# Second-half x factors of a Strassen-like matmul: five of seven loaded, added and split at the turn instead of parked during the first half

## Chip, cores and metric

One NeuronCore of one Trainium2 chip runs the whole program; the other cores are not used. The metric is the device time of one execution in microseconds (us), smaller is better. The profile is one execution of the same program taken by the hardware profiler; its times below are us from the start of its span.

## The reference

The input x has 2048 rows of 512 values, all in fp32. Two branches are computed from it and mixed row by row by a gate.

```python
g = sigmoid((x * gate_w).sum(-1, keepdims=True))
# branch a: linear attention with 32 heads of 16
q, k, v = split_heads(x @ wqkv)                 # wqkv: 512 x 1536
pq, pk = phi(q), phi(k)                         # phi(t) = where(t > 0, t + 1, exp(t)) + 1e-6
kv = einsum("bhsd,bhse->bhde", pk, v); z = pk.sum over s
o  = einsum("bhqd,bhde->bhqe", pq, kv) / (einsum("bhqd,bhd->bhq", pq, z) + 1e-6)
a  = merge_heads(o) @ wo                        # wo: 512 x 512
# branch b: bilinear GLU, F = 1792
b  = ((x @ w_gate) * (x @ w_up)) @ w_down
out = g * a + (1 - g) * b
```

## The kernel before

**Split operands.** Every fp32 matrix that enters a matmul is written as a high part (an fp32r copy, made by ScalarE) and a low part (the rest, made by VectorE: source minus high part). One product then takes three matmuls: high by high, low by high and high by low (`mm3`). Making such a pair is called a split, and in the profile it is an ACT instruction that writes a tile ending in h, and a DVE instruction that writes one ending in l.

**Seven products instead of eight.** For each block of 128 columns of w_gate and w_up (or two such blocks of the q part of wqkv) the kernel computes two 128-column results over two chunks of 512 rows each, as a 2x2 block product in Strassen's manner: seven products of sums of weight blocks with sums of x blocks. The seven sums of x blocks are the x factors, numbered 1 to 7. A factor is 128 partitions x 2 x 512 values, 512 KB, and is held as a high and a low tile: factor 2 in the first half of the tiles xah and xal, 7 in their second half, 3 and 5 in the halves of xbh and xbl, and 1, 4 and 6 in tiles of their own (xc1h, xc1l and so on). Factors 2 and 5 are plain x blocks, the other five are a sum or a difference of two blocks (A1, A2, B1, B2, which are `xp[pair, 0]` to `xp[pair, 3]` in DRAM). A difference is made by a negation on ScalarE (`act(..., scale=-1.0)`) and an accumulating DMA, a sum by the accumulating DMA alone. Accumulating DMAs are issued by GpSimd (POOL), all others by SyncE (SP) with few exceptions.

**Pairs and units.** The 2048 rows are two pairs of 1024. A first phase computes k and the sums for kv and z for all rows and prepares the factors of the first pair. Then come 16 units for the first pair, numbers 0 to 15, and 16 units for the second, 16 to 31. A unit is one set of seven products, 14 of each 16 for the GLU and 2 for q. The seven products run on TensorE in the order 2, 3, 4, 1, 5, 6, 7, with PSUM banks Y, X, R and S as targets (bY, bX, bR, bS in the profile). Between them stand matmuls of the down projection (pdn), from unit 12 and 27 on those of the attention's output (po), and in units 1 to 3 small matmuls that fold kv into wo (pkv, pw). How many down jobs stand at each of four places of a unit is written in the table `shares`. The move from pair to pair, units 15 and 16, is called the turn.

**Order.** Each engine runs its instructions in program order. `later(n, place, fn)` hangs work at a place of unit n, and `do(n, place)` runs it. The places in their order within a unit: high (after product 2), low and e (after product 3), m and c (after product 4), d (before product 1), t (after product 1), s (after product 5), r (after product 6), end (after the unit). So a wait at one place holds up all that stands behind it on that engine.

**Weights.** `w_load(n + 3)` loads the raw weights of a unit (wr) at the end of unit n, `w_add` lets ScalarE copy and negate them and POOL add further blocks, and `w_high` and `w_low` split them (wch, wcl) one unit before they are used.

**The second pair's factors before the change.** While the first pair runs, half a factor at a time is loaded into a tile with the tag cb (three buffers; cbs in the profile) at place s of unit n, added at place c of unit n + 1, and at place e of unit n + 2 handed to `cb_split`. For factors 2, 3 and 4 that splits the half (cbh, cbs) and stores both parts in DRAM tiles xpark; for factors 1, 6 and 7 it stores the sum as it is in xsum. Factor 5 is copied from DRAM to DRAM. The halves run through units 0 to 13 in the order 2, 3, 4, 1, 6, 7. In unit 15, right after a product has used a factor for the last time, `reload` brings the next pair's: both parts of 2, 3 and 4, which are then ready, and the unsplit sums of 1, 5, 6 and 7, which are split in unit 16 at places m, c, t and s.

**Tiles of kv and wo.** In units 2 and 3 `wp_unit` makes four rows of the folded output weights (pw on TensorE, copied by ScalarE into wrow, stored in wraw), and `wp_minus` negates half a row in place and stores it. The wrow tiles share the tag ph, four buffers, with phq, the attention's feature map of a q unit (units 3 and 7).

Of the kernel before, what the change touches and what calls it, by code (L numbers as in the profile page):

```python
# [7 lines left out]
F32 = mybir.dt.float32  # L8
F32R = mybir.dt.float32r
AF = mybir.ActivationFunctionType  # L10
ALU = mybir.AluOpType
# [3 lines left out]
P = 128  # L15
S = 2048
D = 512
# [6 lines left out]
CH = 512  # L24
# [35 lines left out]
def gated_mix(ctx: ExitStack, tc, xt, xp, x, wqkv, wq, wq_add, wo, wgu, wgu_add, wdn, gate_w, out):  # L60
# [3 lines left out]
    dram = ctx.enter_context(tc.tile_pool(name="scratch", bufs=1, space=DRAM))  # L64
# [8 lines left out]
    def act(dst, src, func=AF.Copy, **kw):  # L73
        pin(nc.scalar.activation(dst, src, func, **kw))  # L74

    def tt(dst, a, b, op):
        pin(nc.vector.tensor_tensor(dst, a, b, op=op))  # L77
# [19 lines left out]
    def dma(dst, src):  # L97
        tc.keep_in_program_order(nc.sync.dma_start(dst, src))

    def dma_add(dst, src):  # L100
        tc.keep_in_program_order(nc.gpsimd.dma_start(dst, src, accum_op=ALU.add))  # L101
# [17 lines left out]
    xc = {2: [v[:, 0:2] for v in xa], 7: [v[:, 2:4] for v in xa],  # L119
          3: [v[:, 0:2] for v in xb], 5: [v[:, 2:4] for v in xb], **own}  # L120
# [10 lines left out]
    nc.gpsimd.affine_select(out=m3, in_=m3, compare_op=ALU.is_ge, fill=0.0, base=DH - 1,  # L131
                            pattern=[[DH, P // DH], [0, DH]], channel_multiplier=-1)

    xpark = {i: [dram.tile([P, 2, CH], F32, name=f"xpark{i}{v}") for v in "hl"] for i in (2, 3, 4)}
    xsum = {i: dram.tile([P, 2, CH], F32, name=f"xsum{i}") for i in (1, 5, 6, 7)}

    zpark = dram.tile([KT * KT, P, P // KT], F32, name="zpark")

# [10 lines left out]
    units = len(order) // NPAIR  # L149
# [27 lines left out]
    def w_low(n, part):  # L177
        if n < len(order):
# [5 lines left out]
    SUMS = {1: (A1, B2, 0), 3: (B1, B2, 1), 4: (A2, A1, 1), 6: (A1, B1, 0), 7: (A2, B2, 0), 2: (None, A1, 0),  # L184
            5: (None, B2, 0)}

    def x_load(tile_, pair, i, ks):
        dma(tile_, xp[pair, SUMS[i][1]][:, ks])

    def x_add(tile_, pair, i, ks):  # L190
        one, _, sub = SUMS[i]
        if sub:
            act(tile_, tile_, scale=-1.0)
        if one is not None:
            dma_add(tile_, xp[pair, one][:, ks])
# [4 lines left out]
    with tc.tile_pool(name="p1", bufs=2, reuse_waits="tile") as p1:  # L200
# [11 lines left out]
        for t in range(2 * CH // P):  # L212
            c, i = divmod(t, CH // P)
# [10 lines left out]
        for k in range(KT):  # L224
            raw = raw_of[k]
# [88 lines left out]
        part = phi_k(0, pk0[0])  # L314
        phi_split(*part)
        part = phi_k(1, pk0[1])
# [11 lines left out]
        def cb_load(i):  # L328
            cbs[i] = p1.tile([P, 2, CH], F32, tag="cbs", name="cbs", bufs=3)
            x_load(cbs[i], 0, i, slice(0, 2))  # L330
# [12 lines left out]
        for t in range(LEAD, NT + LEAD):  # L343
# [10 lines left out]
            part = phi_k(*late.pop(0)) if late else None  # L354
# [18 lines left out]
    p2 = ctx.enter_context(tc.tile_pool(name="p2", bufs=1, reuse_waits="tile"))  # L373
# [5 lines left out]
    def later(n, place, fn):  # L379
        at.setdefault((n, place), []).append(fn)  # L380

    def do(n, place):
        for fn in at.pop((n, place), []):
            fn()
# [4 lines left out]
    def down(k):  # L389
# [3 lines left out]
        while ojobs and ojobs[0][0] < passed[0]:  # L393
# [4 lines left out]


    shares = {2: (0, 1, 1, 1), 3: (1, 0, 1, 0), 4: (1, 0, 1, 0), 7: (1, 1, 0, 1), 8: (1, 1, 0, 1), 9: (1, 0, 1, 0)}  # L400
    shares.update({units: (1, 3, 1, 1), units + 1: (1, 1, 1, 0)})
    shares.update({units + m: v for m, v in ((2, (0, 1, 1, 1)), (3, (1, 0, 1, 0)), (4, (1, 0, 1, 0)),
                                             (5, (1, 1, 0, 1)), (6, (1, 1, 0, 1)), (7, (1, 0, 1, 0)),
                                             (15, (1, 1, 0, 1)))})

    def share(n):
        return shares.get(n, (1, 1, 1, 1))

    def unit(n, quad):

        wh, wl = wcs.pop(n)
        bank = {t: psum.tile([P, CH], F32, tag=t, name=f"b{t}") for t in "YXRS"}

        def reload(i):
            if n + 1 == units and i in xpark:
                for src, part in zip(xpark[i], xc[i]):
                    dma(part.bitcast(F32), src)
            elif n + 1 == units:
                hi, lo = xc[i]
                dma(lo.bitcast(F32), xsum[i])  # L420

                def split_there():
                    act(hi, lo.bitcast(F32))
                    tt(lo, lo.bitcast(F32), hi.bitcast(F32), ALU.subtract)

                later(units, {1: "m", 5: "c", 6: "t", 7: "s"}[i], split_there)

        def product(i, to, start=False):
            for k in range(2):
                ks = slice(k * P, (k + 1) * P)  # L430
                mm3(bank[to], (wh[:, SLOT[i], ks], wl[:, SLOT[i], ks]), [v[:, k] for v in xc[i]],
                    start and k == 0, k == 1, not start)
            reload(i)

        m2 = p2.tile([P, CH], F32, tag="t", name="m2")
        cross = p2.tile([P, 2, CH], F32, tag="cross", name="cross", bufs=2)
        product(2, "Y", True)
        act(m2, bank["Y"])
        do(n, "high")
        product(3, "X", True)  # L440

        tt(bank["R"], bank["X"], m2, ALU.subtract)
        do(n, "low")
        do(n, "e")
        many = share(n)
        down(many[0])
        product(4, "Y")
        act(cross[:, 0], bank["Y"])
        do(n, "m")
        do(n, "c")  # L450
        down(many[1])
        do(n, "d")
        if n:
            w_high(n + 1)
        w_add(n + 2)
        product(1, "R")
        t = p2.tile([P, CH], F32, tag="t", name="t")
        tt(t, bank["R"], cross[:, 0], ALU.add)
        if n:
            w_low(n + 1, 0)  # L460
        do(n, "t")
        product(5, "X")
        tt(bank["S"], t, bank["X"], ALU.subtract)
        act(cross[:, 1], bank["X"])
        down(many[2])
        if quad:
            quad(1, 0, cross[:, 0])
        if n:
            w_low(n + 1, 1)
        do(n, "s")  # L470
        down(many[3])
        w_low(n + 1, 2)
        if quad:
            quad(0, 1, cross[:, 1])
        product(6, "R")
        if quad:
            quad(1, 1, bank["R"])
        else:
            hh, hl = hidden()
            tt(cross[:, 1], bank["R"], cross[:, 1], ALU.mult)  # L480
            act(hh[:, 1], cross[:, 1])
        do(n, "r")
        product(7, "S")
        if quad:
            quad(0, 0, bank["S"])
        else:
            tt(cross[:, 0], bank["S"], cross[:, 0], ALU.mult)

            def high(c):
                act(hh[:, c], cross[:, c])  # L490

            def low(c):
                tt(hl[:, c], cross[:, c], hh[:, c].bitcast(F32), ALU.subtract)

            if n + 1 < len(order):

                low(1)
                later(n + 1, "high", lambda: high(0))
                later(n + 1, "low", lambda: low(0))
            else:  # L500

                high(0)
                for c in 1, 0:
                    later(n, f"low{c}", lambda c=c: low(c))
            return hh, hl
# [14 lines left out]
    att = {}  # L520
# [74 lines left out]
    def wp_unit(b):  # L595
        j, r = divmod(b, 2)
        pw = psum.tile([P, D], F32, tag="att", name="pw", bufs=2)
        mm3(pw, [v[:, b] for v in att["kvm"]], att.pop(("woh", b)), True, True)
        att["w", b] = w = p2.tile([P, D], F32, tag="ph", name="wrow", bufs=4)
        act(w, pw)  # L600
        for m in range(2):
            dma(wraw[f"{m + 1}{j + 1}"][:, r], w[:, m * HALF:(m + 1) * HALF])
# [196 lines left out]
    cb = {}  # L799
# [2 lines left out]
        cb[i, k] = p2.tile([P, CH], F32, tag="cb", name="cbs", bufs=3)  # L802
        x_load(cb[i, k], 1, i, k)

    def cb_split(i, k):
        lo = cb.pop((i, k))
        if i in xsum:
            dma(xsum[i][:, k], lo)
            return
        hi = p2.tile([P, CH], F32R, tag="cb", name="cbh", bufs=3)  # L810
        act(hi, lo)
        tt(lo, lo, hi.bitcast(F32), ALU.subtract)
        dma(xpark[i][0][:, k], hi.bitcast(F32))
        dma(xpark[i][1][:, k], lo)

# [6 lines left out]
    later(1, "c", z_there)  # L824
    later(2, "e", kv_split)
    later(2, "c", gate_rows)
    for b, (n, place) in enumerate(((1, "e"), (1, "e"), (2, "end"), (3, "e"))):
        later(n, place, lambda b=b: wo_split(b))
    for b, (n, place) in enumerate(((2, "d"), (2, "s"), (3, "c"), (3, "d"))):
        later(n, place, lambda b=b: wp_unit(b))  # L830
    for b, (n, place) in enumerate(((2, "end"), (3, "e"), (3, "t"), (3, "s"))):
        later(n, place, lambda b=b: wp_minus(b))
    later(3, "d", z_sums)
    for pair in range(NPAIR):
        later(pair * units + 3, "c", lambda pair=pair: dma(
            bmask, gpark[pair * TPP:(pair + 1) * TPP][:, None, :].to_broadcast([TPP, P // TPP, P])))
    for n, (i, k) in enumerate((i, k) for i in (2, 3, 4, 1, 6, 7) for k in range(2)):
        later(n, "s", lambda i=i, k=k: cb_load(i, k))
        later(n + 1, "c", lambda i=i, k=k: x_add(cb[i, k], 1, i, k))
        later(n + 2, "e", lambda i=i, k=k: cb_split(i, k))  # L840
    later(1, "r", lambda: dma(xsum[5], xp[1, SUMS[5][1]]))
    wdr = {}

    ffn = [n for n, u in enumerate(order) if u[1] == "f"]
# [89 lines left out]
```

## Time and profile before

| | |
|---|---|
| time, median of 3 runs | 610.6 us (608.56 to 611.52) |
| the profiled execution's own time | 613.11 us |
| its span, first to last instruction | 611.4 us |
| TensorE busy, share of the span | 598.3 us, 98% |
| VectorE, ScalarE, GpSimd busy | 458.1, 326.7 and 72.9 us |
| moved by DMA | 119.18 MB |

The profiled execution is 2.5 us above the median, and 1.7 us of it lie outside the span. Matmuls are pipelined: a 128x512 matmul is listed with 0.39 us, but the next one starts 0.23 us later when nothing holds it. So a stall of TensorE is read best from the distance of two starts. A number in square brackets behind an instruction is the time that its engine was idle before it, and what ended that.

### The profile page before, as it was taken

The page shows a single profiled execution, that of the slowest core. Times are in us where ns is not written, and L with a number is a line of the kernel's source. Part 1 is how long each engine was busy: PE and PEld are TensorE (multiplying, and loading weights), DVE is VectorE, ACT ScalarE, POOL GpSimd, SP SyncE. Part 2 cuts the span into 40 slices and gives each one's busy share as a digit, 9 for nine tenths or more (in the row PEclk, how much of TensorE's full clock was granted, in tenths as well). Part 3 has the DMA queues.
Part 4 walks back from the last instruction along what each step waited for, and adds up shares of the span by engine and source line. Part 5 has one row for each costly group of instructions (what it writes and reads, how often), then busy time and mean ns, then how long its engine had stood idle before and what let it go on. Part 6 is the DMA issues. An engine that isn't in the chain of part 4 may idle for free.

```text
span 611.4 us, 8215 instructions
## 1 busy us (share of the span) xinstructions
PE 598.3 (98%) x2826; PEld 496.5 (81%) x2826; DVE 458.1 (75%) x729; ACT 326.7 (53%) x572; POOL 72.9 (12%) x93
## 2 busy tenths in 40 slices
PE   8999999998999899999999999999999999999997
PEld 6888888787778688888888878888888888888886
DVE  6977896665687668867879786468778777788855
ACT  3855756578653845443535254965674445453320
POOL 0011100001110102131211021001000013211000
PEclk9999999999999899999999999999999999999999
DMA  9566948767976998999969855387775799966103
GB/s 298 179 189 141 283 103 246 194 185 170 269 192 187 275 267 188 278 301 271 200 171 288 263 154 139 83 232 169 201 184 161 195 225 228 227 177 128 17 1 137
DMA packets 66635, 119.18 MB, mean 195 GB/s; under 512 B 8081, under 2 KB 27025, under 8 KB 66577
## 3 DMA queue, kind: packets, MB, share of 16 engines
q1 hardware_dynamic: 54576, 81.95, 39.7%
q0 software_dynamic: 11728, 36.18, 33.4%
q10 hardware_dynamic: 288, 0.52, 0.3%
q8 instruction: 22, 0.36, 0.2%
q14 instruction: 21, 0.16, 0.1%
HBM read 97.12 MB, written 22.03 MB: 195 GB/s over the span
## 4 chain that ended last, share of the span: by engine, by line
PE 87%; DMA 5%; ACT 3%; DVE 2%; issue 2%; SPq 0%; ACTq 0%; DVEq 0%
PE pdn L68 21%; PE bY L68 13%; PE bX L68 13%; PE bR L68 12%; PE pk L68 7%; PE gt L68 7%; PE po L68 7%; PE bS L68 7%; DMA xpark4l<-cbs 2%; DMA cbs<-in_xp 1%; DMA wr<-in_wgu 1%; DMA wraw-22_101<-wrow 1%; DVE acc L80 1%; DMA wraw<-in_wqkv 1%; ACT wch L74 1%
## 5 line engine op out<-in xcount | busy, mean ns | idle before, releaser
L80 DVE SCALAR_TENSOR_TENSOR acc<-pdn,ocol,acc 128x512 f32<-128x512 f32 (+1 forms) x97 | 71.6, 742 | 25.3 <-PE pdn L68 24.6
L74 ACT ACTIVATE hh<-cross 128x512 fp32r<-128x512 f32 x56 | 35.2, 628 | 100.3 <-DVE cross L77 100.3
L68 PE MATMUL pdn<-dh,hl 128*128 128x512 f32 (+1 forms) x226 | 87.8, 389 | 0.3 <-DVE hl L77 0.3
L68 PE MATMUL pdn<-dh,hh 128*128 128x512 f32 (+1 forms) x226 | 87.9, 389 | 0.0
L68 PE MATMUL pdn<-dl,hh 128*128 128x512 f32 (+1 forms) x226 | 87.8, 389 | 0.0
L77 DVE TENSOR_TENSOR wcl<-wr,wch 128x512 fp32r<-128x512 f32 (+1 forms) x96 | 73.3, 772 | 2.2 <-ACT wch L74 2.2
L74 ACT ACTIVATE wch<-wr 128x512 fp32r<-128x512 f32 (+1 forms) x96 | 60.1, 693 | 0.0
L101 POOL DMA_DIRECT2D wr<-in_wgu_add x28 | 24.1, 860 | 226.4 <-ACT wr L74 108.7
L68 PE MATMUL bX<-xbh,wcl 128*128 128x512 f32 x128 | 50.3, 393 | 0.0
L68 PEld LDWEIGHTS pdn<-dh,hl 128*128 128x128 f32 x226 | 42.6, 188 | 9.4 <-DVE hl L77 0.7
L68 PE MATMUL bX<-xbl,wch 128*128 128x512 f32 x128 | 50.2, 392 | 0.0
L68 PE MATMUL bX<-xbh,wch 128*128 128x512 f32 x128 | 50.0, 391 | 0.0
L68 PEld LDWEIGHTS pdn<-dh,hh 128*128 128x128 f32 x226 | 42.8, 189 | 8.7
L68 PEld LDWEIGHTS pdn<-dl,hh 128*128 128x128 f32 x226 | 42.7, 189 | 8.6
L74 ACT ACTIVATE cross<-bY 128x512 f32<-128x512 f32 x32 | 19.1, 596 | 47.5 <-PE bY L68 47.4
L74 ACT ACTIVATE cross<-bX 128x512 f32<-128x512 f32 x32 | 19.1, 598 | 41.9 <-DVE bS L77 41.9
L77 DVE TENSOR_TENSOR bR<-bX,m 128x512 f32<-128x512 f32 x32 | 22.3, 698 | 24.4 <-PE bX L68 21.7
L77 DVE TENSOR_TENSOR t<-bR,cross 128x512 f32<-128x512 f32 x32 | 22.1, 689 | 24.1 <-PE bR L68 17.6
L77 DVE TENSOR_TENSOR hl<-cross,hh 128x512 fp32r<-128x512 f32 x56 | 38.3, 684 | 0.9
L74 ACT ACTIVATE wr<-wr 128x512 f32<-128x512 f32 x64 | 36.5, 620 | 1.8 <-DMA wr<-in_wgu 1.6
L77 DVE TENSOR_TENSOR acc<-acc,po 128x512 f32<-128x512 f32 x40 | 26.4, 684 | 9.3 <-PE po L68 8.3
L68 PE MATMUL po<-owh,ol 128*128 128x256 f32 x112 | 31.7, 283 | 0.0
(172 smaller groups left out, 1472.6 us busy)
## 6 DMA issues: line engine op xcount, KB each, us to landing
wr<-in_wgu_add POOLq DMA_DIRECT2D x28, 640.0 KB, 6.9
wr<-in_wgu SPq DMA_DIRECT2D x28, 384.0 KB
wdr<-in_wdn SPq DMA_DIRECT2D x28, 256.0 KB
oraw<-opark POOLq DMA_DIRECT2D x20, 256.0 KB, 7.9
xraw<-in_x SPq DMA_DIRECT2D x16, 256.0 KB
terms<-zq SPq DMA_DIRECT2D x16, 256.0 KB
zt<-terms SPq DMA_DIRECT2D x16, 256.0 KB
rb<-den SPq DMA_DIRECT2D x16, 256.0 KB
```

Source lines behind the costliest of these rows:

```text
L68: tc.keep_in_program_order(nc.tensor.matmul(*args, **kw))
L74: pin(nc.scalar.activation(dst, src, func, **kw))
L77: pin(nc.vector.tensor_tensor(dst, a, b, op=op))
L80: pin(nc.vector.scalar_tensor_tensor(dst, a, scalar, b, op0=op0, op1=op1))
L101: tc.keep_in_program_order(nc.gpsimd.dma_start(dst, src, accum_op=ALU.add))
```

## The change

Factors 1, 2, 5, 6 and 7 of the second pair are no longer prepared while the first pair runs. The four x blocks are copied from DRAM to DRAM (xnext) at place r of units 0, 1, 2 and 4. In unit 15 `reload` loads one block into the low tile of each factor after the factor's last use; for 1, 6 and 7 POOL then adds a second block in the tile (at place s of unit 15, e and c of unit 16), and every factor is split in its own tiles (2 at place t, 3 at s and 4 at end of unit 15; 1, 5, 6 and 7 where they were). Factors 3 and 4, the two with a negation, still go through the cb tiles, now in units 5 to 10, are stored unsplit in xsum, and are split at the turn too. The wrow tiles move from the tag ph to cb. Three of the four `wp_unit` stand later, all `wp_minus` later, and one `wo_split` later. In unit 16 one down job moves from before product 1 to before product 6; unit 31 has one down job fewer, which moves behind its last product.

```diff
-    xpark = {i: [dram.tile([P, 2, CH], F32, name=f"xpark{i}{v}") for v in "hl"] for i in (2, 3, 4)}
-    xsum = {i: dram.tile([P, 2, CH], F32, name=f"xsum{i}") for i in (1, 5, 6, 7)}
+    xsum = {i: dram.tile([P, 2, CH], F32, name=f"xsum{i}") for i in (3, 4)}
+    xnext = [dram.tile([P, 2, CH], F32, name=f"xnext{i}") for i in range(4)]
...
-    shares.update({units: (1, 3, 1, 1), units + 1: (1, 1, 1, 0)})
+    shares.update({units: (1, 2, 1, 2), units + 1: (1, 1, 1, 0)})
...
-                                             (15, (1, 1, 0, 1)))})
+                                             (15, (1, 1, 0, 0)))})
...
         def reload(i):
-            if n + 1 == units and i in xpark:
-                for src, part in zip(xpark[i], xc[i]):
-                    dma(part.bitcast(F32), src)
-            elif n + 1 == units:
-                hi, lo = xc[i]
-                dma(lo.bitcast(F32), xsum[i])
-
-                def split_there():
-                    act(hi, lo.bitcast(F32))
-                    tt(lo, lo.bitcast(F32), hi.bitcast(F32), ALU.subtract)
+            if n + 1 != units:
+                return
+            hi, lo = xc[i]
+            raw = lo.bitcast(F32)
+            if i in xsum:
+                dma(raw, xsum[i])
+            else:
+                dma(raw, xnext[SUMS[i][1]])
 
-                later(units, {1: "m", 5: "c", 6: "t", 7: "s"}[i], split_there)
+            def split_there():
+                act(hi, raw)
+                tt(lo, raw, hi.bitcast(F32), ALU.subtract)
+
+            if i in (1, 6, 7):
+                later(*{1: (n, "s"), 6: (units, "e"), 7: (units, "c")}[i], lambda: dma_add(raw, xnext[SUMS[i][0]]))
+            later(*{2: (n, "t"), 3: (n, "s"), 4: (n, "end"), 1: (units, "m"), 5: (units, "c"), 6: (units, "t"),
+                    7: (units, "s")}[i], split_there)
...
-        att["w", b] = w = p2.tile([P, D], F32, tag="ph", name="wrow", bufs=4)
+        att["w", b] = w = p2.tile([P, D], F32, tag="cb", name="wrow", bufs=3)
...
-    def cb_split(i, k):
-        lo = cb.pop((i, k))
-        if i in xsum:
-            dma(xsum[i][:, k], lo)
-            return
-        hi = p2.tile([P, CH], F32R, tag="cb", name="cbh", bufs=3)
-        act(hi, lo)
-        tt(lo, lo, hi.bitcast(F32), ALU.subtract)
-        dma(xpark[i][0][:, k], hi.bitcast(F32))
-        dma(xpark[i][1][:, k], lo)
+    def cb_store(i, k):
+        dma(xsum[i][:, k], cb.pop((i, k)))
...
-    for b, (n, place) in enumerate(((2, "d"), (2, "s"), (3, "c"), (3, "d"))):
+    for b, (n, place) in enumerate(((2, "s"), (3, "e"), (3, "d"), (3, "t"))):
         later(n, place, lambda b=b: wp_unit(b))
...
-    for n, (i, k) in enumerate((i, k) for i in (2, 3, 4, 1, 6, 7) for k in range(2)):
-        later(n, "s", lambda i=i, k=k: cb_load(i, k))
-        later(n + 1, "c", lambda i=i, k=k: x_add(cb[i, k], 1, i, k))
-        later(n + 2, "e", lambda i=i, k=k: cb_split(i, k))
-    later(1, "r", lambda: dma(xsum[5], xp[1, SUMS[5][1]]))
+    for n, (i, k) in enumerate((i, k) for i in (3, 4) for k in range(2)):
+        later(n + 5, "s", lambda i=i, k=k: cb_load(i, k))
+        later(n + 6, "c", lambda i=i, k=k: x_add(cb[i, k], 1, i, k))
+        later(n + 7, "e", lambda i=i, k=k: cb_store(i, k))
+    for i, n in enumerate((0, 1, 2, 4)):
+        later(n, "r", lambda i=i: dma(xnext[i], xp[1, i]))
```

SP's queue in units 5 to 7, before. rb and den belong to the attention's denominator, opark to its output, wr and wdr are weights.

```order
L98 DMA rb<-den_1385 128x1x512 x4
L98 DMA wdr<-in_wdn 128x512
L98 DMA xpark4h<-cbh 128x512
L98 DMA xpark4l<-cbs 128x512
L98 DMA cbs<-in_xp 128x512
L98 DMA opark_984<-rb 128x2x256
L98 DMA opark0-11_988<-phq 128x2x256
L98 DMA opark_985<-rb 128x2x256
L98 DMA wr<-in_wgu 128x768
```

The same stretch after the change.

```order
L98 DMA rb<-den_1362 128x1x512 x4
L98 DMA wdr<-in_wdn 128x512
L98 DMA cbs<-in_xp 128x512
L98 DMA opark_980<-rb 128x2x256
L98 DMA opark0-11_984<-phq 128x2x256
L98 DMA opark_981<-rb 128x2x256
L98 DMA wr<-in_wgu 128x768
```

The two stores of the split factor 4 stood between the weights wdr and the next load into a cb tile, and are gone; that load is now the second one of these tiles and not the seventh.

POOL's queue at the turn, before, from the weight addition for unit 17 on.

```order
L101 DMA oraw<-opark_985 128x512 x2
L101 DMA wr<-in_wgu_add 128x1280
L646 DMA out<-acc 128x512 x3
L101 DMA wr<-in_wq_add 128x1280
L646 DMA out<-acc 128x512 x4
```

And after the change.

```order
L101 DMA wr<-in_wgu_add 128x1280
L101 DMA xc1l<-xnext_87 128x1024
L101 DMA xc6l<-xnext_87 128x1024
L101 DMA xal<-xnext_88 128x1024
L652 DMA out<-acc 128x512 x2
L101 DMA wr<-in_wq_add 128x1280
```

Three accumulating DMAs of 512 KB, for factors 1, 6 and 7, now stand ahead of the first output stores and of the weight addition for unit 18.

ScalarE from the end of unit 15 into unit 16, before.

```order
L74 ACTIVATE oh<-oraw 128x512
L74 ACTIVATE cross<-bX 128x512
L74 ACTIVATE hh<-cross 128x512
L74 ACTIVATE oh<-oraw 128x512
L74 ACTIVATE m_3353<-bY 128x512
```

And after the change.

```order
L74 ACTIVATE oh<-oraw 128x512
L74 ACTIVATE xah<-xal 128x1024
L74 ACTIVATE cross<-bX 128x512
L74 ACTIVATE xbh<-xbl 128x1024
L74 ACTIVATE hh<-cross 128x512
L74 ACTIVATE oh<-oraw 128x512
L74 ACTIVATE xc4h<-xc4l 128x1024
L74 ACTIVATE m_3302<-bY 128x512
```

The high parts of factors 2, 3 and 4 are made here now, each followed by VectorE's low part of the same size; the instructions behind them in unit 16, the splits of 1, 5, 6 and 7 included, stand in the order of before.

More of the change, by code (lines that the diff above doesn't have):

```diff
@@ L826, in gated_mix @@
     later(2, "c", gate_rows)
-    for b, (n, place) in enumerate(((1, "e"), (1, "e"), (2, "end"), (3, "e"))):
+    for b, (n, place) in enumerate(((1, "e"), (1, "e"), (2, "end"), (3, "c"))):
         later(n, place, lambda b=b: wo_split(b))
-    for b, (n, place) in enumerate(((2, "d"), (2, "s"), (3, "c"), (3, "d"))):
+    for b, (n, place) in enumerate(((2, "s"), (3, "e"), (3, "d"), (3, "t"))):
         later(n, place, lambda b=b: wp_unit(b))
-    for b, (n, place) in enumerate(((2, "end"), (3, "e"), (3, "t"), (3, "s"))):
+    for b, (n, place) in enumerate(((3, "e"), (3, "t"), (3, "end"), (4, "c"))):
         later(n, place, lambda b=b: wp_minus(b))
```

## The prediction

> **What bounds the kernel now.** I read the page first, then who waited for whom, then the order of time.
>
> ```profile
> span 611.4 us, 8215 instructions
> PE 598.3 (98%) x2826; PEld 496.5 (81%) x2826; DVE 458.1 (75%) x729; ACT 326.7 (53%) x572; POOL 72.9 (12%) x93
> ```
>
> TensorE is the bound: it is idle for about 13 us. The change removes no matmul and adds none, so all that it can win is TensorE's stalls, and all that it can lose is new ones. TensorE's own waits, by what ended them (total, times, longest):
>
> ```profile
> PE bY L68 <- DVE wcl L77: 3.3, 2, 3.0
> PE bY L68 <- ACT m L74: 2.0, 2, 1.2
> PE pw L68 <- ACT kvmh L74: 0.8, 1, 0.8
> PE bS L68 <- DVE bS L77: 0.7, 1, 0.7
> PE bS L68 <- DVE xal L77: 0.7, 1, 0.7
> PE pdn L68 <- DVE hl L77: 0.3, 1, 0.3
> ```
>
> The first four rows, 6.8 us in six waits, lie in the first pair between 119 and 208 us. The fifth is at the turn, the last at the end of the program. A wait costs more than its idle time, as one of them shows in order of time:
>
> ```profile
> 178.10 0.39 PE L68 MATMUL pdn<-dh,hl 128*128 128x512 f32 x1
> 179.25 0.50 PE L68 MATMUL bY<-xc4h,wch 128*128 128x512 f32 x1 [0.77 <-ACT m L74]
> 179.59 0.40 PE L68 MATMUL bY<-xc4l,wch 128*128 128x512 f32 x1
> 179.83 0.39 PE L68 MATMUL bY<-xc4h,wcl 128*128 128x512 f32 x1
> ```
>
> Two starts, 178.10 to 179.59, take 1.49 us instead of 2 x 0.23: 1.03 lost for 0.77 idle, so 0.26 more per wait. The longest wait, 3.0 us at 204 to 207, also costs clock: in the chain of waits three groups of six matmuls behind it,
>
> ```profile
> 208.70 2.31 PE bX L68 x6
> 211.00 2.02 PE pdn L68 x6
> 214.42 1.37 PE pdn L68 x6
> ```
>
> the first two take 0.94 and 0.65 us more than the third, 1.6 us in all. The first pair thus loses 6.8 + 6 x 0.26 + 1.6 = 10.0 us. (The page "TensorE: Matmul & The Clock Gate" of the Trainium skill, Part 1, says the array falls to half clock after an idle window of about 3.4 us; the trace agrees in kind, at 3.0 us.)
>
> What made the engines late there? ScalarE in order of time, one row of VectorE, and SP's queue:
>
> ```profile
> 148.39 0.60 ACT L74 ACTIVATE phq<-bS 128x512 f32<-128x512 f32 x1 [2.49 <-DMA wraw-22_101<-wrow]
> 168.88 0.63 ACT L74 ACTIVATE cbs<-cbs 128x512 f32<-128x512 f32 x1 [4.34 <-DMA cbs<-in_xp]
> 196.93 0.63 ACT L74 ACTIVATE cbh<-cbs 128x512 fp32r<-128x512 f32 x1 [3.93 <-DMA xpark4l<-cbs]
> 203.44 1.15 ACT L74 ACTIVATE wr<-wr 128x512 f32<-128x512 f32 x2 [1.63 <-DMA wr<-in_wgu]
> ...
> 206.15 0.69 DVE L80 SCALAR_TENSOR_TENSOR phq<-ex,phq 128x512 f32<-128x512 f32 x1 [4.14 <-ACT phq L74]
> ...
> 162.31 0.61 SPq L98 DMA_DIRECT2D cbs<-in_xp  x1
> 184.01 0.92 SPq L98 DMA_DIRECT2D xpark4l<-cbs  x1
> 196.27 0.33 SPq L98 DMA_DIRECT2D cbs<-in_xp  x1
> 198.31 0.50 SPq L98 DMA_DIRECT2D wr<-in_wgu  x1
> ```
>
> Four DMA waits stand inside ScalarE's in-order stream. The first is phq waiting for a buffer of the tag ph that a wrow store still reads. The second and third are the second pair's factors themselves. In the fourth SP could issue nothing from 185 to 196 us, since the next cb load waited for an xpark4 store; the weights behind it went out at 198.3 and landed at 203.4, and the low weights that TensorE waited for at 204 stood on VectorE behind a phq that ScalarE had made late. All four come from the parking or the wrow tiles.
>
> **The change part by part.**
>
> *The parking goes.* In the first pair, half factors cost 12 loads, 10 additions and 12 + 6 stores of 256 KB and a 512 KB copy, 10.5 MB; now 4 copies of 512 KB, 4 loads, 4 additions and 4 stores, 5 MB. On SP 31 issues become 12, on POOL 10 become 4. Splits of halves leave the first pair: six of 0.63 us on ScalarE (the 196.93 row) and as many on VectorE, which lie beside matmuls and win nothing by themselves. What wins is the waits: the 3.93 us wait goes with the split, the 11 us block of SP goes with the stores, and with them the late weights: 3.0 + 0.26 + 1.6 us of TensorE. The 4.34 us wait goes since no half is negated in unit 5 any more; it lies behind the 0.7 wait of bS and the second wait for m. The tag of wrow frees phq (the 2.49 us wait): it lies behind the other two waits for wcl and m, at 144 and 148. The first `wp_unit` goes from place d to s of unit 2, some 4 us later, while kvmh is made when it was: the 0.8 wait goes. So all 10.0 us have their cause removed.
>
> *What comes in their place there.* Factors 3 and 4 are still negated on ScalarE behind a load, now in units 6 to 9. The last of these loads stands behind unit 8's zt loads on SP, as the load of 162.31 stood behind unit 4's. One such wait, 4.34 us long, cost TensorE 0.7 + 0.77 + 2 x 0.26 = 2.0 us. Also the attention's DMAs, which take what they take, have shorter units to hide in, and wrow has three buffers where it had four. So 0 to 2.0 us; I take 1.0, the middle, since unit 9 has no attention work of its own on ScalarE while unit 5 had the late ScalarE of unit 4 before it. The DRAM copies nobody waits for; SP only issues them.
>
> *The turn, splits of 2, 3 and 4.* They were loaded ready, now ScalarE takes 3 x 1.04 and VectorE 3 x 1.22 us between 334 and 349. The rows of ScalarE, VectorE, TensorE and SP there, and the busy time of the engines by stretch (PE, PEld, DVE, ACT, POOL, then granted clock and DMA share):
>
> ```profile
> 336.66 0.60 ACT L74 ACTIVATE cross<-bX 128x512 f32<-128x512 f32 x1 [1.96 <-DVE bS L77]
> 343.67 0.63 ACT L74 ACTIVATE hh<-cross 128x512 fp32r<-128x512 f32 x1 [6.41 <-DVE cross L77]
> 355.73 1.04 ACT L74 ACTIVATE xc6h<-xc6l 128x1024 fp32r<-128x1024 f32 x1
> ...
> 346.41 0.70 DVE L77 TENSOR_TENSOR bR<-bX,m 128x512 f32<-128x512 f32 x1 [0.79 <-PE bX L68]
> 352.10 1.23 DVE L77 TENSOR_TENSOR xc1l<-xc1l,xc1h 128x1024 fp32r<-128x1024 f32 x1 [1.68 <-ACT xc1h L74]
> 357.56 1.22 DVE L77 TENSOR_TENSOR xc6l<-xc6l,xc6h 128x1024 fp32r<-128x1024 f32 x1
> 360.99 1.23 DVE L77 TENSOR_TENSOR xal<-xal,xah 128x1024 fp32r<-128x1024 f32 x1 [0.36 <-ACT xah L74]
> ...
> 362.27 0.51 PE L68 MATMUL bS<-xal,wch 128*128 128x512 f32 x1 [0.67 <-DVE xal L77]
> ...
> 342.03 0.32 SPq L98 DMA_DIRECT2D xc6l<-xsum  x1
> ...
> 322.00:343.00 21.00, 21.00 (x117) 18.30 (x116) 18.83 (x31) 9.29 (x17) 2.02 (x3) 1.00 1.00 296
> 343.00:363.50 20.50, 19.84 (x93) 16.35 (x92) 17.48 (x25) 10.59 (x16) 3.48 (x6) 1.00 0.57 167
> ```
>
> ScalarE has 1.96 and 6.41 us idle just where two of the splits go. VectorE has 21.00 - 18.83 = 2.2 us free in unit 15, then 0.79 and 1.68 before the factor-1 split: 4.7 for 3.7 of new work. It fits, with VectorE up to 1.5 us later in between; its results there are PSUM reads that TensorE wants back several jobs later, so I cost this at nothing. If that cover is short by a whole split, 1.2 us.
>
> *The turn, factors 1, 6 and 7.* Each now needs a load, then POOL's addition, then the split. Factor 6 is the tight one: its load goes out at 342.03 as before, ScalarE reaches its split at 355.73. Loads in busy stretches took 5.1 us (198.31 to 203.44) and 6.6 us (162.31 to 168.88); an addition of 512 KB takes from issue to landing, by the page's list of DMA issues and by the view of the cbs tiles (that one over all their additions), beside the page's row of the down jobs' accumulation:
>
> ```profile
> L80 DVE SCALAR_TENSOR_TENSOR acc<-pdn,ocol,acc 128x512 f32<-128x512 f32 (+1 forms) x97 | 71.6, 742 | 25.3 <-PE pdn L68 24.6
> ...
> cbs<-in_xp POOLq DMA_DIRECT2D x5, 512.0 KB, 7.3
> DMA to landing us min/median/max: 3.6/6.4/9.1
> ```
>
> So it lands at 342.0 + 5.1 to 6.6 + 7.3 = 354.4 to 355.9, just on time. In the old order xc6l started 0.8 us after xc6h was ready, so a landing up to 356.5 costs nothing new. The DMA share of unit 16 was 0.57, which leaves room for the two additions. Moving one down job (one accumulation of 0.74 us on VectorE) behind factor 6's split brings the chain to xal forward by 0.7, against a wait of 0.67 + 0.26 = 0.9. I take a gain of 0.6. Bounds: the whole 0.9 gone; or load and addition at their worst, 6.6 + 9.1, landing at 357.7, a wait longer by 1.2 and a split of VectorE late by 1.2, so 2.4 lost.
>
> By the Trainium skill, "DMA: Bandwidth & Descriptors", the section on the anatomy of a GpSimd DMA, a transfer takes 2.0 us and its bytes over 436 GB/s, 3.2 us here (an estimate from that page), and the turn would gain the whole 0.9 and the time be 600.1; the rows say 7.3 and decide.
>
> *The end.* Unit 31 has one down job less ahead of products 6 and 7, so its last hidden tile is split 1.36 us earlier (six matmuls at 0.23), while TensorE reaches it at the same time as before: the 0.3 + 0.26 goes, 0.6; at least nothing.
>
> **Sum.** -10.0 + 1.0 - 0.6 - 0.6 = -10.2 us: the span goes from 611.4 to 601.2, and the profiled 613.11 to 602.9. That execution lay 2.5 us above the median, so against the median 610.6 the time is 600.4 us.
>
> **Rivals.**
>
> A. *The turn eats part of it.* Factors 6 and 7 land late. For: DMA share 1.00 in unit 15, and VectorE without reserve from 352 to 361. Against: unit 16's share of 0.57, and fewer bytes loaded in unit 15. With the bound above, +3.0 to the sum, 603.4; a wait of over 3 us would add the 1.6 of clock, 605.0.
>
> B. *Half the waits return.* The attention's DMAs (terms, zt, den, rb) stand in the same SP queue in units 4 to 9 and had their own part in the delays; each wait that goes lets the next one show. For: the load of 162.31 was late because of zt, not of parking. Against: the four ScalarE rows name tiles that change. Half of 10.0 back instead of 1.0: 604.4, and up to 607.
>
> C. *Slower.* The turn's chain of load and addition meets a DMA backlog like the one at 184, where a store needed 12.3 us (184.0 to 196.3) to let SP go on. Load and addition of factor 6 at 12.3 each land at 366.6, 10.1 past 356.5; with factor 7's addition behind it in POOL's queue and the clock that is 10.1 + 1.6 + some 2 more, 13.7 lost against 10.2 won: 614. It turns to a loss from a landing at about 363 on. Against: the share of 0.57.
>
> D. *No change*: the removed waits were slack that TensorE finds again at the next DMA, 608 to 612. Against: from unit 18 on, with no factors to park, the second pair runs without a wait until its end.
>
> **Chances.** Forecast 0.60, A 0.15, B 0.15, C 0.05, D 0.05. About 0.5%, 3 us, can be told from no change. Faster: forecast, A and nearly all of B, 0.87; same: D and the rest, 0.08; slower: C, 0.05. Range: the forecast's own bounds are 599 (1.2 less than 600.4 with everything gone and nothing new) to 602.5; the runs differ by up to 2 us from their median; it reaches up through A and most of B: 597.5 to 606.
>
> **What would show it.** In the changed profile TensorE's waits for wcl, m and kvmh in the first pair should be gone or sum to under 1.5 us, no row of ScalarE there should wait over 2 us for a DMA, SP should have no block over 5 us before 230, and units 4 to 8 should take their matmul time. The factor-6 addition should land before 356 on the old scale (about 346 on the new), and the wait for xal at product 7 be under 0.5 us. I am wrong if ScalarE waits at xc6h or xah for POOL's DMA, if zt or wr waits replace those of cbs, or if factor 4's low part holds the third product of unit 16.

## Result and the profile after

The changed kernel takes 603.75 us, the median of 4 runs (603.1 to 604.8), against 610.95 for the kernel before (608.56 to 611.52): 0.9891 of it, 95% interval 0.9861 to 0.9921, 7.2 us less (times are medians, ratios are of means). Two later series, each with 5 runs of it and 16 or 17 of before, gave 602.78 against 611.57 (0.9855, interval 0.9830 to 0.9881) and 602.80 against 611.25 (0.9856, 0.9834 to 0.9878). So the gain is 7 to 9 us. The profiled execution took 603.8 us; it is compared below with the 613.11 of before.

The page after, span and busy time:

```profile
span 602.1 us, 8137 instructions
PE 595.7 (99%) x2826; PEld 496.1 (82%) x2826; DVE 457.7 (76%) x726; ACT 326.0 (54%) x569; POOL 70.4 (12%) x90
```

The work is the same 2826 matmuls; the span is 9.3 us shorter, and DMA moves 113.40 MB instead of 119.18. TensorE's waits, by what ended them (total, times, longest):

```profile
PE warm L68 <- DVE xc1h L124: 1.3, 1, 1.3
PE pdn L68 <- DVE acc L77: 0.9, 1, 0.9
PE bY L68 <- DVE wcl L77: 0.3, 1, 0.3
PE bS L68 <- DVE bS L77: 0.2, 1, 0.2
```

The waits for m, kvmh, xal and hl are gone, that for wcl is down from 3.3 to 0.3; one for acc is new. (The warm row is the start of the program, in both kernels.) Where the 9.3 us came from is read from the start of the first matmul of a unit, and a second profile of before and two more of after show how firm that is:

| us | before | before, 2nd | after | after, 2nd | after, 3rd |
|---|---|---|---|---|---|
| start to unit 0 | 92.20 | 93.06 | 92.47 | 92.92 | 92.27 |
| units 0 to 15 | 251.23 | 250.44 | 243.03 | 243.38 | 242.16 |
| units 16 and 17 (turn) | 33.72 | 33.76 | 33.05 | 33.06 | 33.05 |
| unit 18 to the end | 234.25 | 234.24 | 233.55 | 233.54 | 233.62 |

In the compared pair: +0.27, -8.20, -0.67 and -0.70. Summed over starts, as the prediction measures the loss of one wait, units 0 to 15 lost 10.9 us before (10.1 in the second profile) and lose 2.9 after (3.2 and 2.1). The three places, in TensorE's order of time, each with the matmul ahead of it:

```profile
142.59 0.39 PE L68 MATMUL bY<-xal,wch 128*128 128x512 f32 x1
143.32 0.50 PE L68 MATMUL bY<-xah,wcl 128*128 128x512 f32 x1 [0.35 <-DVE wcl L77]
...
223.02 0.39 PE L68 MATMUL bR<-xc6h,wcl 128*128 128x512 f32 x1
223.64 0.50 PE L68 MATMUL bS<-xah,wch 128*128 128x512 f32 x1 [0.23 <-DVE bS L77]
...
284.10 0.39 PE L68 MATMUL bX<-xbh,wcl 128*128 128x512 f32 x1
285.40 0.50 PE L68 MATMUL pdn<-dh,hh 128*128 128x512 f32 x1 [0.91 <-DVE acc L77]
```

Two of them hang on ScalarE's waits for DMAs:

```profile
219.78 0.63 ACT L74 ACTIVATE cbs<-cbs 128x512 f32<-128x512 f32 x1 [1.17 <-DMA cbs<-in_xp]
...
278.41 0.63 ACT L74 ACTIVATE oh<-oraw 128x512 fp32r<-128x512 f32 x1 [3.27 <-DMA oraw<-opark]
282.13 0.63 ACT L74 ACTIVATE owh<-wraw 128x512 fp32r<-128x512 f32 x1 [2.54 <-DMA wraw<-wraw]
```

The first is the load of the last half factor, which SP issues only behind unit 8's zt loads:

```profile
210.02 2.68 SPq L98 DMA_DIRECT2D zt<-terms  x4
212.74 0.50 SPq L98 DMA_DIRECT2D cbs<-in_xp  x1
```

At the turn, ScalarE's splits of factors 6 and 7, POOL's additions (as issues, then median us from issue to landing), and the busy time of the last stretch in the prediction's form:

```profile
347.81 1.04 ACT L74 ACTIVATE xc6h<-xc6l 128x1024 fp32r<-128x1024 f32 x1
351.32 1.05 ACT L74 ACTIVATE xah<-xal 128x1024 fp32r<-128x1024 f32 x1
...
340.91 0.86 POOL L101 DMA_DIRECT2D xc6l<-xnext  x1 [8.83 <-DMA xc6l<-xnext]
...
xc6l<-xnext POOLq DMA_DIRECT2D x1, 512.0 KB, 6.1
xal<-xnext POOLq DMA_DIRECT2D x1, 512.0 KB, 8.0
...
335.00:355.00 20.00, 20.00 (x94) 16.36 (x94) 18.98 (x27) 11.42 (x17) 4.42 (x7) 1.00 0.91 220
```

Factor 6 lands at 340.91 + 6.1 = 347.0, 0.8 us before ScalarE comes to it, so neither split waits. TensorE has no wait in the view, while the DMA share of unit 16, 0.57 before, is now 0.91 and VectorE has 1.0 us left in 20.

### The profile page after: what moved, and what is told of

Read it like the earlier page. It is cut to its first block, busy times and chain, and to the rows that moved or that the text cites. A ratio compares the mean times of both kernels' runs of the same rounds, so it can differ in the third digit from the quotient of the medians.

```text
span 602.1 us, 8137 instructions
## 1 busy us (share of the span) xinstructions
PE 595.7 (99%) x2826; PEld 496.1 (82%) x2826; DVE 457.7 (76%) x726; ACT 326.0 (54%) x569; POOL 70.4 (12%) x90
## 2 busy tenths in 40 slices
DMA packets 62697, 113.40 MB, mean 188 GB/s; under 512 B 7680, under 2 KB 26624, under 8 KB 62592
## 4 chain that ended last, share of the span: by engine, by line
PE 90%; DMA 5%; DVE 2%; ACT 1%; issue 1%; SPq 0%; DVEq 0%; ACTq 0%
PE pdn L68 23%; PE bY L68 14%; PE bX L68 13%; PE bR L68 13%; PE pk L68 7%; PE gt L68 7%; PE bS L68 7%; PE po L68 6%; DMA wraw<-wraw 2%; DMA cbs<-in_xp 1%; DMA terms<-zq 1%; DMA xlead<-in_xt 1%; SPq L98 0%; PE pkv L68 0%; DVE wcl L77 0%
```

## Experiments

**The kernel before once more**, unchanged.

> The kernel before, once more, with a profile of its own. Theory V: the 13.5 us that TensorE's starts lost in the first profile are mostly waits behind DMAs, which differ from execution to execution; a second profile shows another sum (10 to 13 us) and an own time lower by as much (609 to 612.5), and the waits that differ are those in the first pair. Rival K: the loss is fixed and the profiled execution is high by something outside the span; then the sum is 13.5 +- 0.3 again, and the own time lies 2.5 us above the median once more.

Measured: 611.99 us, median of 12 runs (609.78 to 613.76); the profiled execution 613.23. TensorE's waits in it:

```profile
PE bY L68 <- ACT m L74: 2.2, 2, 1.4
PE pdn L68 <- DVE acc L77: 1.6, 1, 1.6
PE bY L68 <- DVE wcl L77: 1.3, 2, 1.0
PE bS L68 <- DVE bS L77: 1.1, 1, 1.1
```

The rows changed: the 3.0 us wait for wcl is 1.0 here, without the slow matmuls behind it, and there is a wait for acc of 1.6 us in unit 13, the one that seemed new in the changed kernel. So V holds for the waits: the same program has them at other sizes each time. It doesn't hold for the sum. Units 0 to 15 took 0.8 us less here, but the first phase 0.9 more, and the spans are 611.5 and 611.4, so the two executions lost the same in all, as K says. On the time neither expectation held: the own time was above the median again, by 1.2 and not by 2.5.

**The wrow part undone.**

```diff
-        att["w", b] = w = p2.tile([P, D], F32, tag="cb", name="wrow", bufs=3)
+        att["w", b] = w = p2.tile([P, D], F32, tag="ph", name="wrow", bufs=4)
...
-    for b, (n, place) in enumerate(((1, "e"), (1, "e"), (2, "end"), (3, "c"))):
+    for b, (n, place) in enumerate(((1, "e"), (1, "e"), (2, "end"), (3, "e"))):
...
-    for b, (n, place) in enumerate(((2, "s"), (3, "e"), (3, "d"), (3, "t"))):
+    for b, (n, place) in enumerate(((2, "d"), (2, "s"), (3, "c"), (3, "d"))):
...
-    for b, (n, place) in enumerate(((3, "e"), (3, "t"), (3, "end"), (4, "c"))):
+    for b, (n, place) in enumerate(((2, "end"), (3, "e"), (3, "t"), (3, "s"))):
```

> After, but with the wrow tiles in the tag ph again and the places of wo_split, wp_unit and wp_minus as before. Theory S (the parts of the prediction): the waits at pw for kvmh (1.36 us lost by starts) and around unit 4 (0.57 and 1.5) come from these tiles and places, so 2.0 to 3.4 us slower than after, 605.8 to 607.2. Rival P: phq waited for a wrow store only because the parking's stores filled SP's queue; with the parking gone the kvmh wait alone returns, 1.4 us or less, 605.1 or below.

Measured: 605.95 us (604.72 to 606.44), 0.9897 of before (0.9873 to 0.9921), where after had 0.9855 and 0.9856 in the later series: 2.5 us of 611.25, as S said, with overlapping intervals. Against the 0.9891 of the first series it would be 0.4, so the times don't settle what this part is worth. The profile bears S out in kind: two waits of TensorE are back, and ScalarE's phq waits for a wrow store although nothing is parked in those units (the copies to xnext do run there).

```profile
PE pw L68 <- ACT kvmh L74: 0.8, 1, 0.8
PE bY L68 <- ACT m L74: 0.5, 1, 0.5
...
148.46 0.60 ACT L74 ACTIVATE phq<-bS 128x512 f32<-128x512 f32 x1 [1.94 <-DMA wraw-22_97<-wrow]
```

That speaks against P, whose reason was the parking's stores, and its time was missed too. But in this execution the view lists none of the three waits of after, so its units 0 to 15 took 243.18 us, where after took 243.03; waits trade places there, and the 2.5 us of the medians is not accounted for by this one profile.

**The shares undone.**

```diff
-    shares.update({units: (1, 2, 1, 2), units + 1: (1, 1, 1, 0)})
+    shares.update({units: (1, 3, 1, 1), units + 1: (1, 1, 1, 0)})
...
-                                             (15, (1, 1, 0, 0)))})
+                                             (15, (1, 1, 0, 1)))})
```

> After, but with the old down-job places in units 16 and 31. Theory S: the wait for xal at product 7 of unit 16 (0.95 lost by starts) and for hl at the end (0.57) return, 1.0 to 1.6 us slower than after, 604.8 to 605.4. Rival T: with factors 6 and 7 coming by load and addition the old place of the job makes factor 6's low part late as well, 2.5 us or more slower, 606.3.

Measured: 604.54 us (603.32 to 605.19), 0.9874 of before (0.9851 to 0.9898), 0.3 below S's range. Two waits are back at the sizes they had in the kernel before:

```profile
PE bS L68 <- DVE xal L77: 0.7, 1, 0.7
PE pdn L68 <- DVE hl L77: 0.3, 1, 0.3
```

The turn takes 33.75 us and the stretch from unit 18 on 234.34, against 33.05 and 233.55 of after: 0.70 + 0.79, 1.5 us, the whole gain of these two stretches. T is refuted: with the old place of the job factor 6's way of load and addition costs nothing either (it lands 0.4 us ahead of its split).

**Only the way of the factors changed**: both edits above undone together.

> After with both the wrow part and the shares undone: only the way of the second pair's factors is changed. Theory S: of the gain of 7.2 us the parking holds 3.5 to 5, so 606 to 607.5. Rival P (the parking's stores were behind nearly all of it): 5.5 us or more faster than before, 605.4 or less. Rival W (the wrow part is what won): 609 or more.

Measured: 607.34 us (606.33 to 609.9), 0.9926 of before (0.9901 to 0.9952): 4 us faster, inside S's range, near its slow end; W is refuted and P not reached. Units 0 to 15 take 244.12 us in its profile.

**Parking kept, halves unsplit.** The kernel before, but factors 2, 3 and 4 are parked as sums and split at the turn; all loads and additions of the parking stay.

```diff
...
     def cb_split(i, k):
         lo = cb.pop((i, k))
-        if i in xsum:
-            dma(xsum[i][:, k], lo)
-            return
-        hi = p2.tile([P, CH], F32R, tag="cb", name="cbh", bufs=3)
-        act(hi, lo)
-        tt(lo, lo, hi.bitcast(F32), ALU.subtract)
-        dma(xpark[i][0][:, k], hi.bitcast(F32))
-        dma(xpark[i][1][:, k], lo)
+        dma(xsum[i][:, k], lo)
```

> Before, but the halves of factors 2, 3 and 4 are parked unsplit like the others and split at the turn: all 12 loads and 10 additions of the parking remain, the six splits go from the first pair and 12 stores become 6; the wrow tiles and the shares are those of before. Parking alone won about 4 us. Theory Q (SP blocked by the second stores and the splits that wait for them): 3 us or more faster than before, at most 608.3, and SP without a block over 5 us. Rival L (the loads and additions, whose DMAs compete with the attention's): 2 us or less, 609.3 or more.

Measured: 608.24 us, median of 11 (607.25 to 611.0), 0.9944 of before (0.9925 to 0.9963): 3.3 us, so Q, and most of what the parking part wins at all. SP's queue in unit 6:

```profile
182.51 0.46 SPq L98 DMA_DIRECT2D xsum<-cbs  x1
183.01 0.58 SPq L98 DMA_DIRECT2D cbs<-in_xp  x1
188.53 0.38 SPq L98 DMA_DIRECT2D opark<-rb  x1
```

The load that stood for 11 us behind the xpark4 stores goes out 0.5 us after the store. That block cost TensorE 3.3 us by starts at the wait for wcl and 1.6 of slow matmuls in the first profile of before, and 1.3 in the second; here that wait is gone. ScalarE's wait for the load in unit 5 stays, 4.4 us, with 2.1 us of TensorE behind it by starts; these go only with the later units for factors 3 and 4.

**The same with the stores doubled**: each half of factors 2, 3 and 4 is stored a second time, into a tensor that nothing reads.

```diff
...
         dma(xsum[i][:, k], lo)
+        if i in (2, 3, 4):
+            dma(twice[i][:, k], lo)
```

> The kernel with unsplit halves, but every half of factors 2, 3 and 4 is stored a second time, into a tensor that nobody reads: the bytes, the stores and SP's issues of before, without the splits and without the tile cbh. Theory N (the number of buffers: cbh took the third cb tile, so that the next cbs load had to wait for a store): SP has no block over 5 us from 180 to 200, and the time stays within 1 us of the unsplit kernel, 0.993 to 0.996 of before. Rival Y (the bytes of the stores on full DMA queues): the block of about 11 us at 185 returns and the time goes to 0.998 to 1.000 of before.

Measured: 608.22 us, median of 12 (606.85 to 612.18), 0.9952 of before (0.9930 to 0.9973), the time of the kernel with one store.

```profile
182.29 0.43 SPq L98 DMA_DIRECT2D xsum<-cbs  x1
182.76 0.44 SPq L98 DMA_DIRECT2D twice<-cbs  x1
183.25 0.45 SPq L98 DMA_DIRECT2D cbs<-in_xp  x1
```

With 1.5 MB more of stores there is no block, although the DMA engines are busier: their share is 0.94 from 183 to 196 us, against 0.77 during the block of before. In before, SP's own waits from 184 to 197 us name what held it:

```profile
SPq L98 <- DMA xpark4h<-cbh: 11.3, 1, 11.3
```

So N: what held SP for 11 us was that cbh took the third of the three cb tiles, so that the next load had to wait until a store had read one of them; it was not the bytes of the second stores. Why that store took so long isn't shown. Both kernels here also leave out the splits of the halves on ScalarE and VectorE, so how much of the 3.3 us is the tile's is argued from SP's wait, not measured apart. (A kernel with four cb tiles would show it directly; it wasn't tried.)

**More DMA at the turn**: the landing of factor 6 delayed, to price rival A. The copies write tensors that nothing reads.

```diff
...
             else:
+                if i == 6:
+                    for to in spare:
+                        dma(to, xp[1, SUMS[i][1]])
                 dma(raw, xnext[SUMS[i][1]])
```

> After, with two useless 512 KB copies from DRAM to DRAM put on SP's queue just ahead of factor 6's load in unit 15. They delay the load and so factor 6's addition, which landed 0.8 us ahead of its split. Rival A of the prediction priced (the turn eats part of the gain): the addition lands some 4 us later, TensorE waits 1.5 to 4 us in unit 16, 605.5 to 608. Theory F (the turn has slack by VectorE's and ScalarE's idle time, and the other DMAs take the loss): 0.5 us or less.

Measured: 604.08 us (602.88 to 608.39), 0.9891 of before (0.9861 to 0.9922), beside 602.78 of after on the same chip. POOL's addition, ScalarE's split and TensorE:

```profile
343.10 0.86 POOL L101 DMA_DIRECT2D xc6l<-xnext  x1 [10.95 <-PE bY L68]
...
348.80 1.06 ACT L74 ACTIVATE xc6h<-xc6l 128x1024 fp32r<-128x1024 f32 x1 [0.59 <-DMA xc6l<-xnext]
...
353.85 0.39 PE L68 MATMUL bS<-xah,wch 128*128 128x512 f32 x1
354.62 0.50 PE L68 MATMUL bS<-xal,wch 128*128 128x512 f32 x1 [0.39 <-DVE xal L77]
```

The addition lands 13.0 us after the start of unit 16 (335.80), where it landed at 11.5 and 10.8 in the two profiles of after: the copies cost 1.5 to 2.2 us and not the 4 expected, and ScalarE waits for the 0.6 that the slack doesn't cover. Product 7 then starts its second matmul 0.77 us after the first instead of 0.23, and units 16 and 17 take 33.71 us, not 33.06: 0.65 lost, between F (0.5 or less) and A (1.5 or more). The mechanism is A's, and in this one case 0.6 us of lateness cost 0.65 us of TensorE; in its three profiles the changed kernel stands 0.8 to 1.5 us from it. The remaining half of the 1.3 us between the medians isn't in the profiles, whose spans are both 602.9.

**The changed kernel two more times**, the first on the chip of the unsplit halves, the additional DMA and the earlier load (below), the second on that of the doubled stores and the last kernel.

> The changed kernel once more, beside the runs that follow. Theory: 0.986 to 0.991 of before, 603 to 605; in its profile no wait for m or kvmh, the wait of product 7 for bS in unit 9 (0.2 to 1.1) there again, and the wait of a down job for acc in unit 13 (0.9) gone or smaller, since a second profile of before had it (1.6) and the first had not. Rival: the unit-13 wait belongs to the change, and is there again with 0.9 or more.

> The changed kernel a third time, as the measure for the kernel of the same call that moves two things further. 0.985 to 0.990 of before; its profile loses 3 to 5 us by TensorE's starts, with the bS wait of unit 9 somewhere from 0.2 to 1.8.

Measured: the times above, 0.9855 and 0.9856 of before, the first just below its expected range. No wait for acc in unit 13 in either; with the second profile of before, that wait comes and goes with the execution and isn't the change's. The wait for bS in unit 9 was there both times, 1.7 and 0.6 us; the longer one with ScalarE's wait for the cbs load ahead of it:

```profile
221.78 0.63 ACT L74 ACTIVATE cbs<-cbs 128x512 f32<-128x512 f32 x1 [2.68 <-DMA cbs<-in_xp]
...
PE bS L68 <- DVE bS L77: 1.7, 1, 1.7
```

**The last half factor loaded earlier.**

```diff
-        later(n + 5, "s", lambda i=i, k=k: cb_load(i, k))
+        later(*((7, "end") if n == 3 else (n + 5, "s")), lambda i=i, k=k: cb_load(i, k))
```

> After, but the last of the four cbs loads is issued at the end of unit 7, ahead of unit 8's zt loads, and not behind them in unit 8. Theory: ScalarE's wait for that load (1.2 us) goes and with it the losses at product 7 of unit 9 and product 4 of unit 10 (0.2 to 1.5 us): 0.3 to 1.5 faster than after. Rival: the zt loads, now behind a 256 KB load, come later and delay den; no gain, +- 0.3.

Measured: 602.26 us (602.05 to 604.27), 0.9858 of before (0.9833 to 0.9882). In the profile the theory holds: ScalarE does not wait at that place, TensorE's waits after the start are one,

```profile
PE bY L68 <- DVE wcl L77: 0.3, 1, 0.3
```

units 0 to 15 take 240.88 us instead of 243.38, and the span is 600.5, not 602.9. The medians on that chip differ by only 0.5, which these runs don't tell from nothing. The profiled execution of after lay 1.8 us above the median of its 5 runs and this one at its median, so most of the 2.4 between the profiles is that one slow execution. What the earlier load is worth in a typical one the times don't show.

**The earlier load, and VectorE's first phq behind the low weights.** The second edit:

```diff
-        if quad:
-            quad(1, 0, cross[:, 0])
         if n:
             w_low(n + 1, 1)
         do(n, "s")
         down(many[3])
         w_low(n + 1, 2)
         if quad:
+            quad(1, 0, cross[:, 0])
             quad(0, 1, cross[:, 1])
```

> After, with the last cbs load at the end of unit 7, and in q units the first phq of VectorE behind the two low weight parts and not ahead of them. Theory: VectorE stood 2.3 us idle at the end of unit 3 for ScalarE's phq with the low weights queued behind it; now the wait for wcl at product 2 of unit 4 (0.6 us by starts) goes too, and with unit 9's the time is 1.0 to 2.5 us below after, 600.5 to 602. Rival: the wait moves to phq's reader zq or to the PSUM bank that phq frees, no gain beyond +- 0.4.

Measured: 601.77 us (601.11 to 603.8), 0.9849 of before (0.9827 to 0.9871), 1.0 below after on the same chip: the theory's lower edge, and the lowest median of all, though the intervals of the two overlap. VectorE now makes the low weights in the time that it stood idle,

```profile
140.19 1.55 DVE L77 TENSOR_TENSOR wcl<-wr,wch 128x512 fp32r<-128x512 f32 x2
142.56 0.69 DVE L80 SCALAR_TENSOR_TENSOR phq<-ex,phq 128x512 f32<-128x512 f32 x1 [0.82 <-ACT phq L74]
```

and from unit 0 on TensorE has no wait that the view lists. The span is 600.0 us.

## Why the prediction was right, and where it was off

Forecast 600.4, measured 603.75: inside 597.5 to 606.0, and faster, as forecast. By its steps, for the profiled pair:

- *The parking goes, 10.0 us.* Right in the main, and by the cause named: SP's block, the late weights, and the ScalarE waits. The undone parts split it: the factors' way about 4 us, the wrow part 2.5 or less. The loss by starts was 10.9. One term was priced from a single look: SP's block was nearly as long in the second profile, 10.4 us, but TensorE waited 1.0 us for wcl instead of 3.0, with no 1.6 of clock behind it. Half of what is missing there came back as the wait for acc in unit 13, which no step of the prediction names; so that the size fits both profiles of before is partly luck.
- *In their place, 1.0 us.* Mis-sized: 2.9 (3.2 and 2.1 in the other profiles). The wait named there, the last load behind the zt loads, is the one that came, 0.9 us of TensorE by starts in the compared profile and 2.4 in the second. Not named were the rest: 0.6 at unit 4, where phq holds up the low weights, and 1.2 at unit 13, which before has too in one of its two profiles.
- *The turn, -0.6; the end, -0.6.* Measured -0.67 and -0.70. Both come from the moved down jobs alone. The splits of 2, 3 and 4 cost nothing, and factor 6 landed at 347.0, 1 us after the 346 expected, with 0.8 to spare. Unit 16's DMA share went to 0.91 without a loss; the extra copies show how little more it takes.
- *The sum.* Span -9.3 for -10.2, profiled 603.8 for 602.9: 0.9 of the miss. The other 2.5 us is the last step, which failed: to take the whole difference of one profiled execution off the median. That execution of before lay 2.5 us above the median of 3 runs; the changed kernel's lay at its median (603.8 to 603.75), so its forecast should not have been moved down by 2.5. (The later profiles of after lay 1.8 and 0.0 above theirs: the surplus changes with the execution.) The median of 3 was low too: 16 to 18 runs gave 611.25 to 611.57.
- *Rivals.* B happened in part, with 1.9 us more back than the sum had; A lies about 1 us away; C and D are excluded.
- *What would show it.* Right: waits for wcl, m and kvmh together 0.3 us; product 7 doesn't wait. Wrong: SP still stands for more than 5 us five times between 92 and 230, up to 9.1 us, though now for VectorE's results (dl, den, rb, wcl, den) and never for a store; ScalarE still has DMA waits over 2 us in the first pair, the two rows of unit 13 and one of 2.4 us for the weights wr; and factor 6's addition lands 1 us later than said.

## What to carry to other kernels

A DMA queue that stands for ten us may be out of tiles rather than bandwidth: count the tiles of the load's tag before counting bytes, since doubling the stores was free here, and the split that took a third tile was not. Waits on one in-order engine trade places, so price a set of them by the length of the stretch (unit to unit) over two or three profiles, and not by adding up the rows of one. A profiled execution's distance from the median is no constant that the change leaves in place, it was 2.5 and 1.2 us before and 0.05, 1.8 and 0.0 after; a ratio carries it over as well (602.9 / 613.11 of 610.6 is 600.4 again), so widen the range by it.

## What the hardware showed unexpectedly

The accumulating DMAs of 512 KB took 5.5 to 10.6 us from issue to landing at the turn, for the same three transfers in six profiles; the prediction's row of 7.3 was near their middle. (The Trainium skill, "DMA: Bandwidth & Descriptors", the section on the anatomy of a GpSimd DMA, fits 2.0 us and bytes over 436 GB/s; that gives an estimate of 3.2 us for 512 KB, and none of these came near it.) A wait of 2.1 us, the longest after the start in any profile here but one, was followed, after a first gap of 0.34, by matmuls 0.23 to 0.24 us apart, at a granted clock of 1.00. The 3.0 us wait of before was also followed by four at that pace, but then by seven 0.43 us apart, and the granted clock from 208.7 to 212.1 us is 0.52. The Trainium skill, "TensorE: Matmul & The Clock Gate", Part 1, speaks of an idle window of about 3.4 us; these are two single cases, one slowed at 3.0 and one not at 2.1, and no run here shows where between them the limit lies.
